# GpSimd rounds the high half of the second layer's weights from its fifth unit on; loads, splits and values of the attention stand elsewhere

## The chip, the cores and the metric

The kernel runs on one core of a Trainium2 chip. The metric is the device time of one execution in microseconds (us): the median of several executions. Five engines work at once, each through its own instructions in order: TensorE (PE, with PEld for its weight loads), VectorE (DVE), ScalarE (ACT), GpSimd (POOL) and SyncE (SP, which here only issues DMAs). They meet at semaphores.

## The reference

Three parts follow each other, on 2 sequences of 576 tokens (1152 tokens of 512 numbers):

```python
# 1: attention, 8 heads of 64, causal, with a bias from running sums
cum = np.cumsum(np.maximum(s, 0.0), axis=-1)
scores = scale * np.matmul(q, k.transpose(0, 1, 3, 2))
scores = np.where(causal, -1e9, scores + np.minimum(-(cum[..., :, None] - cum[..., None, :]), 0.0))
attn = softmax(scores);  x = np.matmul(attn, v)          # then to (1152, 512)
# 2: a layer of 2048 hidden units with ELU
h = x @ w_in;  x = np.where(h > 0, h, np.exp(np.minimum(h, 0)) - 1) @ w_out
# 3: four experts of 1024 hidden units, weighed by p
for e in range(4):
    out += p[:, e:e + 1] * (np.maximum(x @ w1[e], 0.0) @ w2[e])
```

## The kernel before

The tokens are worked in three groups: 256, 448 and 448. The first group goes alone. Its attention (`attention_first`) is done at once; then it goes through part 2 (`layer1`, 16 units of 128 hidden columns, numbers 0 to 15) and part 3 (32 units, numbers 16 to 47: `NAB` is 16, `NU` is 48). Behind the matmuls of this group the attention of the other 896 tokens is computed, piece by piece (`attention_parts`, run by `Background`). Behind the last units, the first operands of the next stage are made (`early_parts`). From about 240 us on, the two big groups go together through parts 2 and 3 (`both`); the change does not touch that.

**A slot** is one step of the loop for the first group. It runs the up product of one unit (`up1`, `up2`), then `advance(n)`, then the down product of the unit two before. Between them it calls `background(at)`, which runs as many pieces of the attention as the table of points says for that place, from slot 14 on (`BG_FROM`).

**The weights of part 3.** `fetch(n)` (L100) loads a unit's 512 KB into one of 3 buffers `raw`. `prepare(n)` (L107) writes two halves for it into one of 5 buffers `wu`: the high half is the value rounded to the matmul's type (a copy on ACT, L115), and the low half is what the rounding left off, `split_lo` (L92), a subtraction on DVE of two tiles in SBUF. PE multiplies high by high, high by low and low by high (`three`, L718). `advance(n)` (L725) fetches up to unit n+4 and prepares up to unit n+2, so a unit is prepared two slots ahead of its use.

**The attention.** `JOBS` gives eight large jobs (`jobs`, one for each pair of heads and sequence) and four small ones of 128 rows (`small`). A job has items: 128 rows of one head, or a last item of 64 rows of both heads. For an item PE computes the scores (`scores`, `qk`, L563 and L565), DVE adds the mask and takes the maximum (L605), ACT takes the exponential (L612), DVE divides (L585, in `normalise`), PE transposes (L622) three items later (`LATE`), and ACT copies the transposed block into `pt` (L640). After a job's last item, `values` (L663) multiplies with v. `split` (L548 to L551 on ACT, L92 on DVE, and two small loads of the running sums, L545) makes rounded and remaining parts of q and k for one head of a job; it is called in front of the scores of the item before the first that needs it. `load` issues a job's q, k and v in `values` of the job two before; two fills on POOL (L512 and L627) zero the rest of a last chunk.

A scheduler orders each engine's instructions from the program's order and its own estimates; the order is fixed when the program is built.

## Time and profile before

| | |
|---|---|
| median of 3 runs | 684.36 us (681.95 to 688.29) |
| the profiled execution | 683.55 us, of which the profile's span is 681.8 us |
| PE busy | 674.5 us, 99% |
| DVE busy | 583.9 us, 86% |
| ACT busy | 374.5 us, 55% |
| POOL busy | 16.1 us, 2% |
| granted TensorE clock over the span | 1.00 |

The stages in this profile: the first attention until 19 us, part 2 of the first group until 78 us, its part 3 until 240 us, the big groups until 681.8 us. The background attention runs from about 68 to 222 us. A matmul's record lasts until its result is out, while the next one has long begun, so the records overlap, and a short stall of PE is hidden under the tail of the record in front of it.

### The profile page before, as it was taken

How to read it: one execution, taken by the hardware profiler on the slowest of the kernel's cores; microseconds unless marked ns; L12 is line 12 of the kernel's file. 1: busy time of each engine (PE TensorE's matmuls, PEld its weight loads, DVE VectorE, ACT ScalarE, POOL GpSimd, SP SyncE). 2: the span in 40 equal slices, each digit the busy share in tenths (PEclk: the TensorE clock that was granted, in tenths of full speed). 3: DMA queues.
4: the chain of work that ended last, by engine and by line, in shares of the span. 5: the costliest groups of instructions: out<-in, count | busy, mean ns of one | idle time of the engine just before them, and what ended most of it. 6: DMA issues, size and time to landing. Idle time of an engine off the chain costs nothing.

```text
span 681.8 us, 9896 instructions
## 1 busy us (share of the span) xinstructions
PE 674.5 (99%) x3548; PEld 585.3 (86%) x3548; DVE 583.9 (86%) x1139; ACT 374.5 (55%) x763; POOL 16.1 (2%) x47
## 2 busy tenths in 40 slices
PE   9999899999999999999999999999999999999998
PEld 7888788888887888999999888888888888888886
DVE  7999789988977889998999999988888888888765
ACT  6998879888986759554445553333233322223220
POOL 5011000000000000000000000000000000000000
PEclk9999999999999999999999999999999999999999
DMA  8999937755333001111111112111111111110002
GB/s 300 409 365 390 253 121 214 194 169 162 117 108 107 19 31 63 62 62 62 63 62 62 62 36 89 62 62 45 35 47 61 62 62 62 62 62 0 1 0 109
DMA packets 30513, 73.55 MB, mean 108 GB/s; under 512 B 3968, under 2 KB 12544, under 8 KB 30464
## 3 DMA queue, kind: packets, MB, share of 16 engines
q1 hardware_dynamic: 29072, 68.37, 30.4%
q0 software_dynamic: 1248, 4.42, 1.6%
q8 instruction: 28, 0.46, 0.3%
q14 instruction: 21, 0.17, 0.1%
q10 hardware_dynamic: 144, 0.13, 0.1%
HBM read 66.13 MB, written 6.77 MB: 107 GB/s over the span
## 4 chain that ended last, share of the span: by engine, by line
PE 82%; DMA 8%; ACT 4%; DVE 3%; SPq 1%; issue 1%; DVEq 0%; ACTq 0%
PE acc L718 40%; PE att L1053 16%; PE up L1053 12%; PE up L718 6%; DMA pt<-in_qT 2%; PE att L663 2%; DMA wu<-in_w 2%; DMA yl<-in_w 2%; PE acc L622 1%; PE att L622 1%; PE acc L663 1%; DMA cd<-in_w 1%; DMA ox<-in_w 1%; ACT p L612 1%; SPq L145 1%
## 5 line engine op out<-in xcount | busy, mean ns | idle before, releaser
L718 PE MATMUL acc<-w,h 128*128 128x512 f32 (+1 forms) x672 | 170.1, 390 | 0.0
L718 PEld LDWEIGHTS acc<-w,h 128*128 128x128 f32 x672 | 125.9, 188 | 21.4
L1053 PE MATMUL att<-S,top 128*128 128x448 f32 x432 | 99.2, 365 | 0.1
L785 DVE SCALAR_TENSOR_TENSOR xa<-acc,pr,xa 128x512 f32<-128x512 f32 (+1 forms) x105 | 78.1, 745 | 15.2 <-PE acc L718 14.0
L1053 PEld LDWEIGHTS att<-S,top 128*128 128x128 f32 x432 | 80.7, 188 | 9.8 <-DVE u L1079 0.5
L1072 ACT ACTIVATE h<-c 128x448 fp32r<-128x448 f32 x48 | 27.5, 575 | 110.3 <-DVE c L1079 110.1
L718 PE MATMUL acc<-h,w 128*128 128x448 f32 x384 | 86.2, 364 | 0.0
L718 PEld LDWEIGHTS acc<-h,w 128*128 128x128 f32 x384 | 71.5, 188 | 7.1 <-ACT h L1069 0.3
L1053 PE MATMUL up<-x2a,top 128*128 128x448 f32 x288 | 66.3, 367 | 0.2 <-DVE top L92 0.2
L1053 PEld LDWEIGHTS up<-x2a,top 128*128 128x128 f32 x288 | 53.9, 188 | 7.0 <-DVE top L92 0.6
L718 PE MATMUL acc<-wu,gt 128*128 128x512 f32 x192 | 55.4, 403 | 0.0
L718 PE MATMUL up<-yh,wu 128*128 128x256 f32 x256 | 52.7, 287 | 0.0
L1079 DVE TENSOR_TENSOR c<-att,u 128x448 f32<-128x448 f32 x70 | 43.6, 623 | 9.5 <-PE att L1053 8.7
L1073 DVE SCALAR_TENSOR_TENSOR h<-c,h 128x448 fp32r<-128x448 f32 x48 | 29.8, 623 | 18.1 <-ACT h L1072 18.1
L92 DVE TENSOR_TENSOR wu<-raw,wu 128x1024 fp32r<-128x1024 f32 (+1 forms) x33 | 39.0, 1187 | 6.2 <-ACT wu L115 6.2
L718 PEld LDWEIGHTS up<-yh,wu 128*128 128x128 f32 x256 | 42.0, 190 | 1.9 <-issue 0.7
L1072 ACT ACTIVATE h<-up 128x448 fp32r<-128x448 f32 x16 | 8.7, 544 | 55.7 <-PE up L1053 55.7
L718 PEld LDWEIGHTS acc<-wu,gt 128*128 128x128 f32 x192 | 34.0, 189 | 4.9
L612 ACT ACTIVATE p<-p,nm 128x384 f32<-128x384 f32 (+4 forms) x56 | 34.5, 616 | 5.9 <-DVE nm L605 5.3
L718 PE MATMUL up<-yl,wu 128*128 128x256 f32 x128 | 36.5, 285 | 0.1
L1169 DVE TENSOR_TENSOR ox<-acc,ox 128x448 f32<-128x448 f32 x56 | 34.3, 618 | 2.7 <-PE acc L718 2.4
L115 ACT ACTIVATE wu<-raw 128x1024 fp32r<-128x1024 f32 (+1 forms) x33 | 33.6, 1027 | 3.2 <-PE acc L718 3.1
(234 smaller groups left out, 1217.0 us busy)
## 6 DMA issues: line engine op xcount, KB each, us to landing
raw<-in_w SPq DMA_DIRECT2D x35, 512.0 KB
wr<-in_w SPq DMA_DIRECT2D x10, 1024.0 KB
wr<-in_w SPq DMA_DIRECT2D x12, 512.0 KB
wu<-in_w SPq DMA_DIRECT2D x10, 512.0 KB
k<-in_kT SPq DMA_DIRECT2D x16, 288.0 KB
w_dec<-wu POOLq DMA_DIRECT2D x8, 512.0 KB, 7.3
wr<-w_dec SPq DMA_DIRECT2D x4, 1024.0 KB
cd<-in_w SPq DMA_DIRECT2D x6, 512.0 KB
```

The source lines that it names most:

```text
L92: return DVE.tensor_tensor(out=lo, in0=x, in1=hi.bitcast(F32), op=ALU.subtract)
L115: ACT.activation(t[:, 0, r], x[:, r], AF.Copy)
L612: ACT.activation(p, p, AF.Exp, bias=nm, scale=-1.0, accum_out=sm)
L622: PE.transpose(pt[:cb[c + 1] - cb[c], m, :], p[:, cb[c]:cb[c + 1]], ident)
L663: PE.matmul(o[64 * j:64 * j + 64, qs:nq], job["v"][:, c, 64 * j:64 * j + 64], job["pt"][:, j, c, qs:nq], start=c == 0, stop=c == n_c - 1)
L718: PE.matmul(o, a[m], b[n], start=first and i == 0, stop=last and i == 2)
L785: DVE.scalar_tensor_tensor(out=o_sb, in0=o, scalar=pr[:, i, e:e + 1], in1=o_sb, op0=ALU.mult, op1=ALU.add)
L1053: PE.matmul(bank, tops[q][:, m, op, cs], x[:, n, c], start=first and c + i == 0, stop=c == 1 and i == 2, skip_group_check=True)
L1072: ACT.activation(h[:, 0, u, cs], c, AF.Relu)
L1073: DVE.scalar_tensor_tensor(out=h[:, 1, u, cs], in0=c, scalar=0.0, in1=h[:, 0, u, cs].bitcast(F32), op0=ALU.max, op1=ALU.subtract)
L1079: DVE.tensor_tensor(out=t, in0=a, in1=b, op=ALU.add)
L1169: DVE.tensor_tensor(out=y[:, c, cs], in0=o, in1=y[:, c, cs], op=ALU.add)
```

## The change

1. `prepare`: from unit 20 on (the fifth of part 3), the high half is made by a copy on POOL in place of the copy on ACT. That is 28 of 32 units. The low half stays on DVE.
2. Loads at the start of the background attention: the running sums of the first two splits are asked for first (`load_sums`), then the small jobs' q, k and v, and then the raw weights of units 16, 17 and 18. Before, units 16 and 17 were asked for ahead of the small jobs' tensors. `advance` fetches and prepares nothing before slot 14.
3. `split` is called behind the scores of an item and for the item after the next, one item earlier than before. A job's q and k (`load_both`) are asked for right after the second split of the job two before; v (`load_values`) in `values`, as before.
4. `values` of a job stands behind the transposes of the next item; before, it stood in front of them.
5. `up2` of unit 16: the four matmuls with the low half of the activations (`yl`) come last.
6. `keep_warm(9)` in place of `keep_warm(7)`: two more matmuls without use at the start.

```diff
-                ACT.activation(t[:, 0, r], x[:, r], AF.Copy)
+                if n < NAB + 4:
+                    ACT.activation(t[:, 0, r], x[:, r], AF.Copy)
+                else:
+                    POOL.tensor_copy(t[:, 0, r], x[:, r])
...
-        keep_warm(7)
+        keep_warm(9)
...
             with tc.issue_after(last.ins):
-                fetch(fetch_at[0])
-            fetch_at[0] += 1
+                while fetch_at[0] < NAB + 3:
+                    fetch(fetch_at[0])
+                    fetch_at[0] += 1
...
+            if j == 1 and job.get("next"):
+                load_both(job["next"])
...
-            if job in jobs and jobs.index(job) + 2 < len(jobs):
-                load(jobs[jobs.index(job) + 2])
+            if job["next"]:
+                load_values(job["next"])
...
             if small:
+                load_sums(items[0])
+                load_sums(items[1])
...
-                        if c[2] and n + 1 < len(items):
-                            split(items[n + 1])
                         scores(it, c)
+                        if c[2] and n + 2 < len(items):
+                            split(items[n + 2])
...
-            if ready:
-                parts.append(ready.pop())
+            due = ready[:]
+            ready.clear()
...
+            parts += due
...
-        while fetch_at[0] <= min(n + 4, NU - 1):
+        while n > BG_FROM - 1 and fetch_at[0] <= min(n + 4, NU - 1):
...
-        while prepare_at[0] <= (NAB if n == NAB - 3 else min(n + 2, NU - 1)):
+        while n > BG_FROM - 1 and prepare_at[0] <= min(n + 2, NU - 1):
...
-            for c in range(NCC):
-                three(o, halves(t, 0, dm(c)), (yh[:, c], yl[:, c]), c == 0, c == NCC - 1)
+            terms = [(c, i) for c in range(NCC) for i in range(3)]
+            if n == NAB:
+                terms.sort(key=lambda a: a[1] == 1)
```

POOL, from the last write of decoded weights on, before (`v` and `pt` are fills of the attention's tiles, `w_dec` is a store):

```order
L188 DMA w_dec<-wu 128x1024 x8
L512 MEMSET v 64x128 x2
L627 MEMSET pt 64x2x64 x2
L512 MEMSET v 64x128
L627 MEMSET pt 64x2x64
```

and the same place in the changed kernel:

```order
L191 DMA w_dec<-wu 128x1024 x8
L515 MEMSET v 64x128 x2
L118 CAST wu<-raw 128x1024 x2
L647 MEMSET pt 64x2x64 x2
L118 CAST wu<-raw 128x1024 x3
L515 MEMSET v 64x128
L647 MEMSET pt 64x2x64
L118 CAST wu<-raw 128x1024 x3
```

The copies of units 20 and 21 come ahead of the first two fills of `pt`, those of units 22 to 24 behind them, and so on to unit 47; each waits for the fills in front of it.

PE at the first scores of the background attention (`kh,qs` and `kl,qb`), in slots 14 to 16, before (L813 is the down product of part 2, L823 its up product):

```order
L823 MATMUL up<-xf,ox 128x256 x4
L563 MATMUL att<-kh,qs 128x128
L813 MATMUL acc_467<-gt,wu 128x256
L813 MATMUL acc_468<-gt,wu 128x256
L813 MATMUL acc_469<-gt,wu 128x256
L813 MATMUL acc_470<-gt,wu 128x256
L563 MATMUL att<-kh,qs 128x128
L813 MATMUL acc_467<-gt,ox 128x256
L565 MATMUL att<-kl,qb 128x128
```

and in the changed kernel (L838, L848, L583 and L585 are the same lines of code):

```order
L848 MATMUL up<-xf,ox 128x256 x4
L838 MATMUL acc_469<-gt,wu 128x256
L838 MATMUL acc_470<-gt,wu 128x256
L838 MATMUL acc_471<-gt,wu 128x256
L838 MATMUL acc_472<-gt,wu 128x256
L583 MATMUL att<-kh,qs 128x128
L838 MATMUL acc_469<-gt,ox 128x256
L585 MATMUL att<-kl,qb 128x128
```

The first scores stand four matmuls later on PE.

SP behind the last coded weights (`xa`), before (`raw` is a unit's weights of part 3; `pt` here the small jobs' q, k and v):

```order
L145 DMA xa<-in_w 128x1024 x3
L104 DMA raw<-in_w 128x1024 x2
L478 DMA pt<-in_qT 128x4x128
L481 DMA pt<-in_kT 64x4x128 x4
L483 DMA pt<-in_v 128x512
L104 DMA raw<-in_w 128x1024
```

and in the changed kernel:

```order
L148 DMA xa<-in_w 128x1024 x3
L544 DMA qb<-rows_d 4x4x128
L544 DMA kl<-rows_d 4x4x128
L544 DMA qb<-rows_d 4x4x128
L544 DMA kl<-rows_d 4x4x128
L481 DMA pt<-in_qT 128x4x128
L484 DMA pt<-in_kT 64x4x128 x4
L486 DMA pt<-in_v 128x512
L104 DMA raw<-in_w 128x1024 x3
```

Two loads of weights moved from in front of the small jobs' tensors to behind them, and four loads of a few KB in front.

## Rows read from the trace of the kernel before

**Rows 1.** The page: busy time by engine; GB/s moved in 40 slices of 17 us.
```profile
PE 674.5 (99%) x3548; PEld 585.3 (86%) x3548; DVE 583.9 (86%) x1139; ACT 374.5 (55%) x763; POOL 16.1 (2%) x47
...
GB/s 300 409 365 390 253 121 214 194 169 162 117 108 107 19 31 63 62 62 62 63 62 62 62 36 89 62 62 45 35 47 61 62 62 62 62 62 0 1 0 109
```

**Rows 2.** Busy time by stretch: from:to, length, engines (instructions), clock, DMA share, GB/s.
```profile
95.00:140.00 45.00, 44.21 (x302) 36.92 (x304) 41.43 (x110) 41.60 (x101) 1.04 (x6) 1.00 0.69 191
140.00:222.00 82.00, 81.94 (x563) 68.25 (x559) 67.25 (x177) 67.89 (x162) 1.69 (x8) 1.00 0.43 132
222.00:240.00 18.00, 18.00 (x110) 16.00 (x109) 16.47 (x25) 12.13 (x19) 0.00 (x0) 1.00 0.02 9
```

**Rows 3.** Timeline of PE around its four longest stalls: start, us, line, idle before.
```profile
70.84 0.33 PE L563 MATMUL att<-kh,qs 128*128 128x128 f32 x1 [0.64 <-ACT kh L549]
...
75.14 0.33 PE L563 MATMUL att<-kh,qs 128*128 128x128 f32 x1 [0.68 <-DVE nm L605]
...
84.08 0.30 PE L622 MATMUL att<-ident,p 128*128 128x128 f32 x1 [0.56 <-DVE p L585]
...
105.52 0.41 PE L572 MATMUL att<-kl,qb 68*128 68x384 f32 x1 [0.53 <-ACT gt L907]
```

**Rows 4.** Timelines of SP, ACT and DVE ahead of the first two stalls.
```profile
49.97 0.99 SPq L104 DMA_DIRECT2D raw<-in_w  x2
51.07 0.42 SPq L478 DMA_DIRECT2D pt<-in_qT  x1
...
67.62 0.63 ACT L548 ACTIVATE qs<-pt 64x512 fp32r<-64x512 f32 x1 [2.51 <-DMA pt<-in_qT]
...
73.65 1.23 DVE L92 TENSOR_TENSOR wu<-raw,wu 128x1024 fp32r<-128x1024 f32 x1 [0.52 <-ACT wu L115]
74.79 0.28 DVE L605 CUSTOM_DVE_ANT_0 p<-att,mask 128x128 f32<-128x128 f32 x1
```

**Rows 5.** Waits of weight loads, 62 to 240 us: us, times, longest; those with releaser.
```profile
PEld att L563 <- DVE nm L605: 1.3, 2, 1.1
...
PEld att L663 <- ACT pt L640: 1.0, 3, 0.6
...
PEld acc L653 <- ACT pt L640: 0.2, 1, 0.2
```

**Rows 6.** POOL by line and form: count, busy us, mean ns, idle before.
```profile
L244 POOL CAST rows<-cum 16x576 fp32r<-16x576 f32 x1 | 0.7, 654 | 0.9 <-DVE cum L234 0.9
```

**Rows 7.** DVE and ACT by line and form, 95 to 222 us.
```profile
L92 DVE TENSOR_TENSOR wu<-raw,wu 128x1024 fp32r<-128x1024 f32 x23 | 28.1, 1222 | 3.7 <-ACT wu L115 3.7
L115 ACT ACTIVATE wu<-raw 128x1024 fp32r<-128x1024 f32 x23 | 24.2, 1051 | 3.2 <-PE acc L718 3.1
```

**Rows 8.** Timeline near 5 us: two equal POOL instructions, and DVE beside them.
```profile
4.89 0.42 DVE L305 TENSOR_TENSOR cump<-cum,cump 16x256 fp32r<-16x256 f32 x1
5.11 0.30 POOL L221 TENSOR_SCALAR_AFFINE_SELECT maskp<-maskp 64x64 f32<-64x64 f32 x1
5.34 0.48 DVE L231 SCALAR_TENSOR_TENSOR bias<-bias,eight 16x320 f32<-16x320 f32 x1
5.46 0.47 POOL L221 TENSOR_SCALAR_AFFINE_SELECT maskp<-maskp 64x64 f32<-64x64 f32 x1
```

**Rows 9.** DVE's time in 95:140 by line: first L92, then L585.
```profile
95.00:140.00 45.00, 18.52 (x22) 1.00 0.69 191
...
95.00:140.00 45.00, 7.59 (x18) 1.00 0.69 191
```

**Rows 10.** Timelines of POOL and PE near 100 us: fills, and unit 22's first two matmuls.
```profile
97.67 0.35 POOL L627 MEMSET pt<- 64x128 f32 x2 [33.66 <-DVE qs L92]
...
102.89 0.28 PE L718 MATMUL up<-yh,wu 128*128 128x256 f32 x1
103.01 0.28 PE L718 MATMUL up<-yl,wu 128*128 128x256 f32 x1
```

**Rows 11.** Timeline of PE at the start of the program.
```profile
0.78 3.33 PE L389 MATMUL att<-const-float32-0.0 128*128 128x128 f32 x14 [0.78 <-PEq L1266]
```

More of the change, by code (lines that the diff above doesn't have):

```diff
@@ L521, in load, with of, load_sums @@
                                                 in_=v[b, cb[i]:cb[i + 1], r])
+        for i, job in enumerate(jobs):
+            job["next"] = jobs[i + 2] if i + 2 < len(jobs) else None
+        def of(it):
+            job, j = it["job"], 1 if it["j"] is None else it["j"]
+            return job, j, small if job["q1"] == 128 else [job]
+        def load_sums(it):
+            job, j, together = of(it)
+            heads = slice(job["b"] * H + 2 * together[0]["hp"] + j,
+                          job["b"] * H + 2 * together[-1]["hp"] + j + 1, 2)
+            job[j, "sums"] = []
+            for tag, r, a in (("qb", slice(0, 4), job["q0"]), ("kl", slice(2, 6), 0)):
+                t = sb([68, len(together) * (job["q1"] - a)], tag, 2, F32R)
+                job[j, "sums"].append(t)
+                with late():
+                    SP.dma_start(
+                        out=t[64:].bitcast(F32).rearrange("r (h n) -> r h n", h=len(together)),
+                        in_=rows_d[heads, r, a:job["q1"]].rearrange("h r n -> r h n"))
         def split(it):
-            job, j = it["job"], 1 if it["j"] is None else it["j"]
+            job, j, together = of(it)
             if (j, "q") in job:
                 return
+            if (j, "sums") not in job:
+                load_sums(it)
             mine, other = (slice(64 * i, 64 * i + 64) for i in (j, 1 - j))
-            together = small if "all" in job else [job]
-            heads = slice(job["b"] * H + 2 * together[0]["hp"] + j,
-                          job["b"] * H + 2 * together[-1]["hp"] + j + 1, 2)
             if "all" in job:
@@ L540, in split @@
             kh = sb([128, k.shape[-1]], "kh", 2, F32R)
-            qb = sb([68, q.shape[-1]], "qb", 2, F32R)
-            kl = sb([68, k.shape[-1]], "kl", 2, F32R)
-            for t, r, a in ((qb, slice(0, 4), job["q0"]), (kl, slice(2, 6), 0)):
-                with late():
-                    SP.dma_start(
-                        out=t[64:].bitcast(F32).rearrange("r (h n) -> r h n", h=len(together)),
-                        in_=rows_d[heads, r, a:job["q1"]].rearrange("h r n -> r h n"))
+            qb, kl = job[j, "sums"]
             ACT.activation(qs[mine], q, AF.Copy)
@@ L683, in start @@
                 for job in jobs[:2]:
-                    load(job)
+                    load_both(job)
+                    load_values(job)
             split(items[0])
```

24 lines of the change are left out of this document (14 added, 10 removed).

## The prediction

> **What bounds the kernel now.** I read the page first. PE is busy for 674.5 of 681.8 us [rows 1], and its clock is granted in full in every stretch below. The number and size of useful matmuls stay the same, so this change can only take away time in which PE stands, or add some. Next I looked at the stretches: from 140 to 222 us PE is busy for 81.94 of 82 us, from 222 to 240 for all 18, and from 95 to 140 for 44.21 of 45 [rows 2]. So the attention behind part 3 is hidden, and what can be won lies early, between 70 and 110 us. The reader is to see in the timeline of PE its four longest stalls: 0.64 us at 70.84, 0.68 at 75.14, 0.56 at 84.08 and 0.53 at 105.52 [rows 3]. They make 2.41 us. A matmul's record lasts beyond the start of the next (one of 0.28 us is followed after 0.12 us [rows 10]), so each stall is about 0.16 us longer than its bracket; I take 3.05 us for the four. The waits of the weight loads, which also show what hides under a tail, name a releaser for 7.7 us in 14 lines between 62 and 240 us, the four stalls among them [rows 5]. That is about the most that the change can win.
>
> The second thing to see is how full the helpers are. From 95 to 140 us DVE works 41.43 and ACT 41.60 of 45 us; from 140 to 222 us they work 67.25 and 67.89 of 82; from 222 to 240 us 16.47 and 12.13 of 18 [rows 2]. DVE has 3.57, 14.75 and 1.53 us left.
>
> **The copy on POOL.** One copy takes 1.05 us on ACT [rows 7]. The trace has no copy of 128x1024 on POOL. Its nearest row is a conversion of the same kind over 576 columns, 0.654 us [rows 6], which scaled by columns is 1.16 us; that is the upper end, since a fixed part would not scale. ACT's own 1.05 us is the lower. I take 1.1 us. 28 copies leave ACT, 29 us in all, and POOL takes 31 us of a queue that had 16 us in all [rows 1]. The 32 units take 162 us (78 to 240), 5 us each, so POOL keeps up. The last eight copies, with no fill between them, can even run ahead of ACT's old times.
>
> ACT is not what PE waits for from 110 us on, so most of the 29 us buys nothing. It buys something where ACT's queue makes PE or DVE late: DVE waits 3.7 us in all for these copies [rows 7], and the stall at 105.52 us ends behind ACT.
>
> **What the copy costs DVE.** Here the trace speaks against the change. Near 5 us POOL runs two equal instructions on 64x64 elements [rows 8]. The first takes 0.30 us, the second 0.47 us. Beside the second, DVE runs an instruction with two inputs in SBUF from 5.34 to 5.82 us, and POOL ends at 5.93, just behind it. The first likewise ends at 5.41, just behind a DVE subtraction that ends at 5.31. So the two engines seem to exclude each other there. The Trainium skill (SBUF — State Buffer, Who interferes with whom) says that a DVE instruction with two SBUF inputs and a GpSimd instruction that reads SBUF block each other fully, whoever starts first; by that rule each copy may hold DVE for its whole length, and the trace agrees as far as these two rows go.
>
> The price here: while a copy holds, DVE can go on until its next subtraction of SBUF tiles. In 95:140 these subtractions (L92) fill 18.52 of 45 us, and the divisions of the probabilities (L585) another 7.59 [rows 9]. Whether the latter collide no row shows. If only L92 does, a copy costs DVE 0.41 x 1.1 = 0.45 us; with both 0.58 x 1.1 = 0.64 us. The bounds are 0 (POOL waits each time, which harms nobody, as units are ready some us early) and 1.1 us. I take 0.6. Nine copies fall in 95:140, fourteen in 140:222, three in 222:240, two before. At 0.6 DVE needs 5.4 us more where it had 3.57, 8.4 where it had 14.75, 1.8 where it had 1.53: 2.1 us too much. Scores are three items ahead of their transposes, and DVE has room again behind 140 us, so not all of a late DVE reaches PE. I take **+1.4 us**.
>
> **Loads in another order.** The small jobs' tensors stand behind 1 MB of weights that is not needed until 78 us [rows 4]. ACT waits 2.51 us for them and starts the first split at 67.62 us; at the 390 GB/s of the fourth slice (51 to 68 us) [rows 1] 1 MB is 2.7 us. So the first split can start some 2.5 us earlier. Behind the loads stand the weights of units 16 to 18; the total ahead of the large jobs' loads is the same. On PE the first scores now also stand behind four down products, so the 0.64 us stall has cover from both sides. The second stall has another cause: DVE makes the low half of unit 17 at 73.65 us, itself waiting 0.52 us for ACT, and the maximum for which PE waits comes only at 74.79 [rows 4]. In the changed order the first maxima stand in front of that subtraction. I count both stalls gone: 0.64 + 0.68 + 2 x 0.16, **-1.6 us**.
>
> **Splits earlier, values later.** The stall at 105.52 us is at a score whose operands come from ACT late in a full queue [rows 3]. The split is called one item earlier and ACT is freer: **-0.7 us**. The stall at 84.08 us waits for the division of a first item; that chain starts earlier but has the same length: half of it, **-0.35 us**. `values` in front of the next transposes waits 1.0 us in three times for ACT's copy of the last block [rows 5]; behind them, ACT has that time. With the other small waits (14 lines, 7.7 us, less some 4.6 in the four stalls and the loads around them) some 3 us are left; I count a third, **-1.1 us**. Unit 16's `yl` matmuls last: a wait of 0.3 us among these. The q and k loads that move cost nothing: they are covered by the two items of lead.
>
> **Two more warm matmuls.** Seven are 14 records in 3.33 us [rows 11], so two more are four records, 0.95 us. Below, 0: the first sums come from DVE and may be the later ones. I take **+0.3 us**.
>
> **The sum.** -1.6 - 0.7 - 0.35 - 1.1 + 0.3 + 1.4 = -2.05 us. The profiled execution took 683.55 us, so 681.5; its time lies 0.8 us under the median of the runs, so I state the forecast against the median: 684.36 - 2.05 = **682.3 us**.
>
> **The rivals.** *DVE becomes the bound.* If a copy holds DVE for its whole 1.1 us, DVE needs 9.9, 15.4 and 3.3 us more in the three stretches, 6.3 + 0.65 + 1.8 = 8.8 us above what it had left. If PE then waits for all of it, and only the two early stalls go: 684.36 + 8.8 + 0.3 - 1.6 = **691.9 us**. For it speaks the second select [rows 8]; against it that POOL must find DVE between two subtractions, and that DVE's own idle time has waits for ACT in it that go away. It decides from about 0.7 us a copy on, where the loss equals the gain. Chance 0.12.
>
> *All waits go.* If all 7.7 us of waits with a releaser vanish [rows 5] and DVE is not held, 684.36 - 7.7 + 0.3 = **677.0 us**. Against it: waits of a full pipeline move more often than they vanish. Chance 0.12.
>
> *Nothing happens.* The stalls go and come back in other places, since PE's order is new throughout and DVE is as late as ACT was before: 684.4 us, give or take 1.5. Chance 0.2.
>
> *POOL's queue is late.* The copies of units 22 to 24 stand behind two fills that ended at about 98.0 us before [rows 10]. A copy (1.1) and a subtraction (1.22) later it is 100.4 us, and unit 22's first matmul came at 102.89. Even a fill 2.5 us later only meets PE; beyond that PE loses us for us: at 6 us late, some 3.5 us, 685.8. Chance 0.06; it ends within 1%.
>
> **How the numbers follow.** The forecast (0.5) and the rivals make one: 0.5 + 0.12 + 0.12 + 0.2 + 0.06. About 1% (6.8 us) is what a measurement of this kernel can tell from no change. Under 677.5 lies the second rival, over 691.2 the first; the rest is within 1%: 0.12, 0.76, 0.12. The range reaches to the all-waits case and to a lock that costs 0.9 us a copy: 676.5 to 690.0 us. The forecast's own range is 679.5 to 685.
>
> **What would show it.** POOL: 28 copies of 1.05 to 1.2 us, some longer because they wait behind DVE. DVE: subtractions of 128x1024 with means well over 1.22 us, and busy over 43 of 45 us early on. PE: no stall over 0.5 us from 68 to 77 us, stalls between 77 and 110 us of half their sum, and no more than 1.5 us between 110 and 240 us. ACT: some 4 us less for every 20 us until 240 us. The forecast is wrong if PE shows new waits for DVE of more than 3 us behind 95 us, if the copies take 2 us, or if anything behind 245 us moves.

## The result and the profile after

The changed kernel takes 688.93 us (median of 10 runs, 687.41 to 689.76); the kernel before took 683.52 us beside it. The ratio is 1.0071, with a 95% interval from 1.0056 to 1.0087: **0.7% slower**, where 682.3 us was forecast. That is within the 1% that was called no change, and inside the range, but on the other side of the old time and 6.6 us from the forecast.

The page after (span 686.3 us), busy times beside [rows 1], and the chain of work that ended last, by engine:

```profile
PE 677.0 (99%) x3552; PEld 585.4 (85%) x3552; DVE 592.9 (86%) x1139; ACT 350.2 (51%) x735; POOL 50.9 (7%) x75
...
PE 72%; DVE 15%; ACT 5%; DMA 4%; issue 3%; DVEq 0%; SPq 0%; ACTq 0%
```

The same chain in the kernel before:

```profile
PE 82%; DMA 8%; ACT 4%; DVE 3%; SPq 1%; issue 1%; DVEq 0%; ACTq 0%
```

DVE's share of it has risen from 3 to 15%. Busy time by stretch in the changed kernel (the columns of [rows 2]: PE, PEld, DVE, ACT, POOL), with the stretch of the first two stalls ahead:

```profile
62.00:78.00 16.00, 15.89 (x78) 13.59 (x76) 11.56 (x34) 11.32 (x28) 0.52 (x3) 1.00 1.07 307
95.00:140.00 45.00, 42.89 (x304) 36.08 (x302) 43.25 (x103) 33.34 (x86) 11.73 (x15) 1.00 0.62 184
140.00:222.00 82.00, 80.22 (x543) 66.04 (x543) 70.59 (x181) 55.53 (x149) 17.31 (x22) 1.00 0.44 128
222.00:240.00 18.00, 17.34 (x105) 13.67 (x103) 14.61 (x19) 8.64 (x15) 5.82 (x3) 1.00 0.09 29
```

From 62 to 78 us PE now stands for 0.11 us: the early stalls [rows 3] are gone. From 95 to 140 us PE has lost 1.3 us of work against [rows 2], and from 140 to 222 us, where it had stood for 0.06 us, it now stands for 1.8. ACT is 8 and 12 us emptier in these two stretches, and it did not help. DVE is fuller, 43.25 of 45 us and 70.59 of 82, with no instruction more (its page count is 1139, as before).

The same as a running account: how much later than in the kernel before the same matmul starts, in us (from the two traces; "unit n" is the first up product of unit n of part 3):

| place (us before) | changed kernel |
|---|---|
| first up product of part 2 (19.3) | +1.00 |
| last down product of part 2 (78) | -0.70 |
| unit 24 (117) | +0.55 |
| unit 32 (162) | -0.02 |
| unit 43 (224) | +2.67 |
| end of part 3 (240) | +4.20 |
| end | +4.58 |

So the start loses 1.0, the stretch from 20 to 78 us wins 1.7, and then three stretches lose: 1.25 up to unit 24, 2.7 between units 32 and 43, and 1.5 in the last units. Between units 24 and 32 the changed kernel loses nothing; behind part 3 it loses 0.4.

Two of these pieces are those of one execution only. The start of part 2 differs from profile to profile: over all kernels of this document its first up product comes between 0.23 us earlier and 1.00 later than in the kernel before with nine warm matmuls, and between 0.31 earlier and 0.60 later with seven. And up to unit 24 two kernels with the same order of instructions there (the change with seven warm matmuls, and with its last four copies on ACT, both below) lose 2.4 and 2.7 us where the changed kernel loses 1.25. The 2.7 between units 32 and 43 are the same in all three.

Which instructions got longer is seen in DVE's groups by line and form from 78 to 246 us; the first two rows are of the order edits with the copies left on ACT (the first experiment), the next two of the changed kernel (x count | busy us, mean ns | idle before):

```profile
L92 DVE TENSOR_TENSOR kl<-k,kh 64x576 fp32r<-64x576 f32 x16 | 12.0, 748 | 0.3
L599 DVE TENSOR_SCALAR sm<-sm 128x2 f32<-128x2 f32 x27 | 4.4, 162 | 5.2 <-ACT p L629 5.1
```

```profile
L92 DVE TENSOR_TENSOR kl<-k,kh 64x576 fp32r<-64x576 f32 x16 | 14.3, 894 | 0.3
L602 DVE TENSOR_SCALAR sm<-sm 128x2 f32<-128x2 f32 x27 | 7.5, 279 | 4.4 <-ACT p L632 4.4
L603 DVE RECIPROCAL sm<-sm 128x2 f32<-128x2 f32 x27 | 4.3, 161 | 0.4
L92 DVE TENSOR_TENSOR wu<-raw,wu 128x1024 fp32r<-128x1024 f32 x30 | 36.4, 1216 | 1.4 <-POOL wu L118 1.0 <-ACT wu L116 0.4
```

The subtractions of k and the additions to the softmax sums have means up by 146 and 117 ns; the reciprocals and the large weight subtractions have not. Wherever I speak of *lengthening* below, it is the sum, over DVE's instructions from 78 to 246 us, of what each takes over the median of the same operation and form without POOL copies, where that is more than 0.05 us. For the changed kernel it is 11.3 us in 21 instructions, the longest single one 0.84 us: **0.40 us a copy**.

### The profile page after: what moved, and what is told of

Read it like the earlier page. It is cut to its first block, busy times and chain, and to the rows that moved or that the text cites. A ratio compares the mean times of both kernels' runs of the same rounds, so it can differ in the third digit from the quotient of the medians.

```text
span 686.3 us, 9910 instructions
## 1 busy us (share of the span) xinstructions
PE 677.0 (99%) x3552; PEld 585.4 (85%) x3552; DVE 592.9 (86%) x1139; ACT 350.2 (51%) x735; POOL 50.9 (7%) x75
## 4 chain that ended last, share of the span: by engine, by line
PE 72%; DVE 15%; ACT 5%; DMA 4%; issue 3%; DVEq 0%; SPq 0%; ACTq 0%
PE acc L743 35%; PE att L1082 16%; PE up L1082 12%; DVE wu L92 3%; DVE p L625 2%; PE up L933 2%; DVE p L605 2%; DMA k<-in_kT 2%; DVE kl L92 1%; DMA pt<-in_kT 1%; ACT z L177 1%; DVE qs L92 1%; DMA xa<-in_w 1%; PE att L683 1%; DVE gt L937 1%
## 5 line engine op out<-in xcount | busy, mean ns | idle before, releaser
L118 POOL CAST wu<-raw 128x1024 fp32r<-128x1024 f32 x28 | 33.9, 1213 | 97.6 <-PE acc L743 57.9
L92 DVE TENSOR_TENSOR wu<-raw,wu 128x1024 fp32r<-128x1024 f32 (+1 forms) x33 | 38.9, 1184 | 2.1 <-ACT wu L116 1.1
```

The costliest lines, as they stand in the source:

```text
L92: return DVE.tensor_tensor(out=lo, in0=x, in1=hi.bitcast(F32), op=ALU.subtract)
L118: POOL.tensor_copy(t[:, 0, r], x[:, r])
```

## The experiments

Each expectation was written before its run. The names in them: READ LOCK or LOCK, DVE's instructions on SBUF are held while POOL reads SBUF; START, the two warm matmuls shift everything; LATE HALF, the rounded half is ready too late; DVE BOUND, each us more on DVE costs PE a us; SLACK, DVE's idle time takes it; CHAIN, only time in the softmax chain counts; BURSTS, only long single waits count; ORDER, in the first four expectations that the moved splits, loads and values themselves cost, and in those of the last runs that the planner (the scheduler) put instructions in another succession, because copies on POOL leave ACT free in its plan. The ratios are against the kernel before, run beside each set; its medians are 683.52 us in the first section and for the change, and 683.82 to 683.91 in the others. So a difference of two runs from different sets is uncertain by some 0.4 us.

### Which part of the change costs

**Copies back on ACT, all else changed.**

```diff
-                if n < NAB + 4:
-                    ACT.activation(t[:, 0, r], x[:, r], AF.Copy)
-                else:
-                    POOL.tensor_copy(t[:, 0, r], x[:, r])
+                ACT.activation(t[:, 0, r], x[:, r], AF.Copy)
```

> The changed kernel with the 28 rounded halves made by ACT again; everything else of the change stays. Theory LOCK (POOL's copies hold DVE's subtractions and divisions, and PE then waits for DVE): 688.9 less the 5.9 us that the trace of the change lost behind 78 us, so 683.0 to 684.5; DVE beside no POOL work goes back to 1.22 us for 128x1024 and 0.75 us for 64x576 in every instance. Theory ORDER (the moved splits, loads and values put PE's pieces where they wait): 688 to 689, POOL's copies cost nothing. Theory START (two more warm matmuls shift everything by 1.0 us): the start stays 1.0 us late in this run under both.

Measured: 681.69 us, ratio 0.9969 [0.9957, 0.9981]. The copies on POOL cost 688.93 - 681.69 = **7.2 us**; everything else together wins 1.8. More comes back than LOCK expected (683.0 at the least), and the start of part 2 is 0.36 us late in this profile, not 1.0.

**The kernel before with POOL's copies alone** (the opposite edit, in the old order of loads and splits).

> The kernel before with one edit: POOL makes the rounded halves from the fifth unit of part 3 on. Theory LOCK: 683.5 plus 4 to 6 us, 687.5 to 689.5, with DVE instructions of two SBUF inputs lengthened beside the copies and those that read PSUM not. Theory ORDER: 683 to 684.5, since nothing but the engine of the copies moves.

Measured: 689.94 us, ratio 1.0100 [1.0082, 1.0117]; lengthening 12.2 us. The copies cost 6.4 us there too, 0.4 us more than LOCK's range, so it is not their meeting with the new order of loads and splits.

**The change with seven warm matmuls.**

```diff
-        keep_warm(9)
+        keep_warm(7)
```

> The changed kernel with seven warm matmuls at the start as before. Theory START: 1.0 us less than the changed kernel, 687.9, and part 2's first up product at 19.3 us in place of 20.3. If the warm matmuls only shift a wait that is there anyway, 688.9.

Measured: 688.08 us, ratio 1.0063 [1.0051, 1.0075]. By the medians the two warm matmuls cost 0.85 us. The two profiled executions, 688.36 us with seven and 688.10 with nine, do not show it.

**The order edits alone**: copies on ACT and seven warm matmuls.

> The loads, splits and values of the change with neither POOL's copies nor the two warm matmuls. LOCK and START together: 683.5 less the 1.7 us won between 62 and 78 us, 681 to 683. ORDER: 687.5 to 688.

Measured: **680.85 us**, ratio 0.9959 [0.9948, 0.9971]. This is faster than both kernels, and 0.15 us under the range that was expected. Between it and the first run the two warm matmuls cost 0.84 us by the medians of five runs each. In the mean of all profiles part 2 starts 0.44 us later with nine warm matmuls than with seven, so their cost lies between about 0.4 and 0.85 us. From 140 to 222 us PE is busy throughout, and the early stalls are gone:

```profile
62.00:78.00 16.00, 15.90 (x79) 13.60 (x78) 11.53 (x33) 11.30 (x29) 0.41 (x2) 1.00 1.08 295
140.00:222.00 82.00, 82.00 (x563) 68.28 (x560) 67.91 (x178) 68.16 (x163) 1.39 (x8) 1.00 0.45 133
```

### What about the copies costs: late, or in DVE's way?

**A spare copy in the kernel before**: ACT makes the rounded half as ever; POOL copies the same tile once more into the place of the low half, which DVE then overwrites.

```diff
                 ACT.activation(t[:, 0, r], x[:, r], AF.Copy)
+            if n >= NAB + 4:
+                POOL.tensor_copy(t[:, 1, r], x[:, r])
```

> The kernel before, ACT still making the rounded halves; beside that POOL copies each unit's raw weights (from unit 20 on) into the place of the low half, which DVE's subtraction then overwrites. Nothing useful is moved. Theory READ LOCK (a POOL instruction that reads SBUF and a DVE instruction that reads two SBUF tensors exclude each other, and PE waits for the late DVE): 683.5 plus 5 to 8 us, 688.5 to 691.5, DVE instructions lengthened by 10 to 13 us in sum. Theory LATE HALF (the loss comes from weights that are ready late because POOL's queue stands in front of the subtraction): the same loss here and in the run with fills.

Measured: 690.62 us, ratio 1.0091 [1.0061, 1.0121]; lengthening 15.5 us, where 10 to 13 was expected. The order on ACT, DVE and PE is line for line that of the kernel before, and nothing that a matmul reads comes from POOL. But DVE's subtraction has to wait for the spare copy, since it overwrites it, so this run alone does not tell the lock from that wait. The next one does.

**A spare fill**: the same with `POOL.memset(t[:, 1, r].bitcast(F32), 0.0)` in the copy's place. The subtraction waits for it in the same way.

> As the run before, but POOL fills that place with zeros (it only writes, 128x1024) in place of copying. READ LOCK: subtractions are not lengthened; at most the divisions of SBUF by a scalar are, so 683.5 to 685.5. LATE HALF: as with the copies, 688 to 691, since the subtraction waits for POOL in the same way.

Measured: 684.42 us, ratio 0.9995 [0.9976, 1.0014]. The order is again that of the kernel before. DVE's groups from 78 to 246 us, as above:

```profile
L92 DVE TENSOR_TENSOR kl<-k,kh 64x576 fp32r<-64x576 f32 x16 | 11.9, 746 | 0.7 <-ACT kh L551 0.4
L584 DVE TENSOR_SCALAR sm<-sm 128x2 f32<-128x2 f32 x26 | 8.0, 307 | 3.3 <-ACT p L614 3.2
```

Not one subtraction of two SBUF tiles is longer (64x576: 748 ns in the mean without POOL's work, 746 here, where nine of the 16 meet a fill). Some of the additions to the sums (159 ns alone, seven of the 26 here between 418 and 865) and some divisions still are, 6.2 us in all. So POOL has to read SBUF to hold a subtraction. DVE idles for the fills as long as for the copies (1.5 us in two times, 1.3 in one), and yet the time is only 0.55 us over that of the kernel before, which the interval does not tell from nothing: LATE HALF falls as the main cause of the 6.7 us, and READ LOCK stands.

**More DVE work that the planner knows of.** First 28 subtractions of 128x256 (0.42 us each, 11.7 us) ahead of the units' low halves; then 28 multiplications by 1.0 of up to 128x384 (9.0 us in its trace) between reciprocal and division in the softmax. Both in the kernel before, without work for POOL.

```diff
+            if n >= NAB + 4:
+                split_lo(t[:, 1, 0:256], x[:, 0:256], x[:, 0:256])
```

> The kernel before with a subtraction of 128x256 more on DVE for each unit from 20 on, in front of the unit's own subtraction, which overwrites it: 28 x 0.42 = 11.7 us of DVE, about what the copies cost it, and no POOL. Theory DVE BOUND (between 78 and 245 us what DVE does more reaches PE for the most part, though DVE stands 15 to 20 percent of that time): 683.5 plus 5 to 8 us. Theory SLACK (my reckoning before the run: DVE's idle time takes it): 683.5 to 685.5.

Measured: 685.23 us, ratio 1.0015 [0.9998, 1.0032].

```diff
             DVE.reciprocal(sm, sm)
+            m = norm[-1][:, :min(384, norm[-1].shape[-1])]
+            DVE.tensor_scalar(m, m, 1.0, None, op0=ALU.mult)
```

> The kernel before, with one more DVE multiplication by 1.0 of up to 128x384 (about 0.42 us, 28 of them, 11 us or a little less in all) in the chain of each pair of softmax rows, between the reciprocal and the divisions; GpSimd has no new work. The DVE time is that of the earlier kernel with 28 more subtractions ahead of the weight splits, which lost 1.3 us; only the place differs. CHAIN (time on DVE counts when it stands in the chain from maximum to division to transposes, on which PE waits; that is where the lock falls): a loss of 4 to 6 us, 688 to 690. BURSTS (only the size of single waits counts, 0.42 us is absorbed wherever it stands): 685 to 686.

Measured: 683.71 us beside 683.91, ratio 0.9990 [0.9978, 1.0003]. DVE BOUND and CHAIN fall: 11.7 us more on DVE cost 1.4, which the interval does not quite tell from nothing, and 9.0 us cost nothing, which is less than BURSTS expected too. But in both kernels the planner also changed the order of DVE and PE around the new instructions. Whether time that the planner knows of is absorbed because it is planned for, or because no piece is over 0.42 us, these two runs do not show. In the profile of the first, 0.8 of the 2.5 us are lost ahead of 78 us, where DVE has no new work yet.

**Copies in quarters**, in the changed kernel.

```diff
-                    POOL.tensor_copy(t[:, 0, r], x[:, r])
+                    for c in range(0, 1024, 256):
+                        POOL.tensor_copy(t[:, 0, c:c + 256], x[:, c:c + 256])
```

> The changed kernel with each copy on POOL cut into four of 256 columns. If the two engines exclude each other for one whole instruction, DVE waits at most 0.3 us for each in place of 1.05; DVE's lengthening should fall from 11.3 us to 5 to 8 us and the time from 688.9 to 685.5 to 687.5. If POOL takes the turn again for each quarter ahead of DVE, or more turns cost what shorter ones win, 688 to 690.

Measured: 687.86 us, ratio 1.0048 [1.0033, 1.0064], between the two ranges that were expected. The lengthening falls to 6.2 us and no single one is over 0.25 us, so DVE is held for the length of POOL's instruction, not for the tile. Only 1.1 us comes back, though: four quarters take longer than one copy (1.44 us in this row), and DVE, whose next instruction in line is that unit's subtraction, now idles for them, 4.9 us in eight times against 1.0 in two. Timeline of POOL, then of DVE, in this kernel:

```profile
194.86 1.44 POOL L119 CAST wu<-raw 128x256 fp32r<-128x256 f32 x4 [1.79 <-issue]
...
196.33 1.22 DVE L92 TENSOR_TENSOR wu<-raw,wu 128x1024 fp32r<-128x1024 f32 x1 [0.50 <-POOL wu L119]
197.47 0.68 DVE L606 TENSOR_SCALAR p<-p,sm 128x256 f32<-128x256 f32 x2
```

The division behind it is what PE's transposes wait for, 0.5 us at 199.14. The run shows the lock's form; it doesn't measure its price.

### Where it is lost, and by which way

**Copies of the last four units back on ACT**, the rest changed.

```diff
-                if n < NAB + 4:
+                if n < NAB + 4 or n >= NU - 4:
                     ACT.activation(t[:, 0, r], x[:, r], AF.Copy)
```

> The changed kernel with the copies of the last four units (44 to 47) back on ACT. In the changed kernel those of 45 to 47 ran 1.9 to 2.0 us on GpSimd and their splits ended 1.3, 0.4 and 1.0 us behind the start of the unit's first up product, where before they ended 0.3 to 1.6 us ahead of it; the stretch from 222 us to the end of the third part lost some 1.5 us. If these late copies are what the end of the stage loses, the median falls by 1.2 to 1.8 us, to about 687.3, and no up product behind 222 us waits for DVE's L92 more than 0.2 us. If the end loses by something else, 688.7 to 689.2.

Measured: 686.99 us, ratio 1.0041 [1.0024, 1.0058], 1.9 us below the change. From unit 43 to the end of part 3 it loses 0.0 us (the changed kernel 1.5). This loss is late copies after all: timeline of POOL, DVE and PE at the end of part 3 in the changed kernel:

```profile
226.72 1.88 POOL L118 CAST wu<-raw 128x1024 fp32r<-128x1024 f32 x1 [6.58 <-PE acc L743]
229.53 1.92 POOL L118 CAST wu<-raw 128x1024 fp32r<-128x1024 f32 x1 [0.93 <-PE acc L743]
232.35 2.02 POOL L118 CAST wu<-raw 128x1024 fp32r<-128x1024 f32 x1 [0.90 <-PE acc L743]
...
230.81 1.53 DVE L92 TENSOR_TENSOR top<-ox,top 128x512 fp32r<-128x512 f32 x2
232.25 1.21 DVE L92 TENSOR_TENSOR wu<-raw,wu 128x1024 fp32r<-128x1024 f32 x1
...
233.52 0.51 PE L933 MATMUL up<-yh,wu 128*128 128x256 f32 x2 [0.54 <-DVE wu L92]
```

The copies take 1.9 to 2.0 us here instead of 1.04, beside DVE's long instructions with two SBUF inputs: it is POOL's turn to be held. The weight slots come free only as PE ends a unit, so there is no time ahead, and the split of unit 45 at 232.25 is late by what PE then stands.

**Without the addition of 1e-9** to the softmax sums (28 instructions of 128x2, which leave a sum of at least 1 as it is), with seven warm matmuls: once with the copies on POOL, once on ACT.

```diff
-            DVE.tensor_scalar(sm, sm, 1e-9, None, op0=ALU.add)
             DVE.reciprocal(sm, sm)
```

> The changed kernel with seven warm matmuls and without the addition of 1e-9 to the sums of the softmax (28 instructions of 128x2, which leave a sum of at least 1 as it is). These additions were the instructions that met a copy most often: 12 of 28, 159 ns alone, 429 ns in the mean beside one. Without them the lock has 3.3 of its 11.3 us less to fall on, and the chain is 28 x 0.16 us shorter. ADDITIONS CARRY IT: the distance to the same kernel with the copies on ACT falls from 7.2 us to 4 or less, so about 684. ANY INSTRUCTION WILL DO (the lock then holds the next two-input or SBUF instruction): the distance stays at 6.5 to 7.2, so 687 to 688.

> The order edits alone (copies on ACT, seven warm matmuls), without the same 28 additions of 1e-9: the other half of the pair. 4.5 us of DVE time go from the chain of the softmax. CHAIN: where 0.42 us more per pair costs much, 0.16 us less should give something back, 0.5 to 1.5 us below 680.85, so 679.4 to 680.4. BURSTS and SLACK: PE waits there for nothing that 0.16 us shortens, 680.6 to 680.9.

Measured: 684.72 us, ratio 1.0012 [1.0003, 1.0021], and 681.76, ratio 0.9968 [0.9955, 0.9980]. With the additions gone the copies cost 3.0 us instead of 7.2, as ADDITIONS CARRY IT says; but the lengthening fell only from 11.5 to 9.6 us, since divisions took the hold that the additions no longer took, and without the additions the order on DVE and PE changed as well (the stall of 1.2 us at 183 us, below, is 0.6). So the pair does not show that the additions carry it. The second kernel is 0.9 us slower than with the additions (680.85), outside both ranges that were expected for it; since its order changed too, it says nothing on CHAIN or SLACK.

**Only ten copies on POOL**, those of units 25 to 34, in the stretch where the changed kernel lost nothing.

```diff
-                if n < NAB + 4:
+                if not NAB + 9 <= n < NAB + 19:
                     ACT.activation(t[:, 0, r], x[:, r], AF.Copy)
```

> The changed kernel with only the copies of units 25 to 34 on GpSimd (10 of 28; they ran from 113 to 162 us), the others on ACT. In that stretch the changed kernel had the most lengthening of DVE (4.3 us between 117 and 160 us) and lost nothing there against the copies on ACT (0.05 us from unit 24 to unit 32). If the place decides (DVE has room in this stretch), 681.5 to 682.5. If each copy costs its share of 7.2 us, 684.3.

Measured: 682.20 us, ratio 0.9970 [0.9950, 0.9989], 0.5 us over the copies on ACT where the share of ten copies would be 2.6. The lengthening is 4.7 us, and it costs PE 0.7 us by the running account. So the place counts for more than the us of lengthening.

**LOCK without the new succession**: the order edits with nine warm matmuls and the copies on ACT (681.69), plus a spare copy on POOL as above. The order on ACT, DVE and PE is line for line that of the first run.

> The order edits with nine warm matmuls and the copies on ACT (681.69 measured), and GpSimd copies each of the 28 tiles once more into the place of the low half, ahead of DVE's subtraction. The order on ACT, DVE and PE is line for line that of the kernel without the spare copies; only GpSimd works more. LOCK: the loss of the change and more, as with the spare copies in the kernel before (6.7 us there), 687 to 689. ORDER: the lock alone costs less than half of 7.2, so 683.5 to 685. If the two causes add up, this loss and that of the kernel with fills make about 7.

Measured: 689.59 us, ratio 1.0072 [1.0047, 1.0096]: **7.9 us** for the lock, 0.6 us more than its range. Since the two kernels have the same succession, an instruction can be set beside itself. DVE, and then PE, first with the copies on ACT alone:

```profile
99.17 0.15 DVE L599 TENSOR_SCALAR sm<-sm 128x2 f32<-128x2 f32 x1
99.36 0.49 DVE L92 TENSOR_TENSOR qs<-q,qs 64x320 fp32r<-64x320 f32 x1
...
99.96 0.73 DVE L92 TENSOR_TENSOR kl<-k,kh 64x576 fp32r<-64x576 f32 x1
100.62 0.84 DVE L602 TENSOR_SCALAR p<-p,sm 128x576 f32<-128x576 f32 x2
...
101.27 0.63 PE L639 MATMUL att<-ident,p 128*128 128x128 f32 x4
```

and with the spare copies (POOL first):

```profile
99.51 2.03 POOL L117 CAST wu<-raw 128x1024 fp32r<-128x1024 f32 x2
102.72 1.33 POOL L117 CAST wu<-raw 128x1024 fp32r<-128x1024 f32 x1 [1.19 <-DVE kl L92]
...
100.26 0.31 DVE L601 TENSOR_SCALAR sm<-sm 128x2 f32<-128x2 f32 x1
100.60 1.27 DVE L92 TENSOR_TENSOR qs<-q,qs 64x320 fp32r<-64x320 f32 x1
...
101.99 0.73 DVE L92 TENSOR_TENSOR kl<-k,kh 64x576 fp32r<-64x576 f32 x1
102.64 1.61 DVE L604 TENSOR_SCALAR p<-p,sm 128x576 f32<-128x576 f32 x2
...
103.29 0.63 PE L641 MATMUL att<-ident,p 128*128 128x128 f32 x4 [0.94 <-DVE p L604]
```

Two copies run from 99.51 to 101.54. The addition and the subtraction of q that fall beside them take 0.31 and 1.27 us where they took 0.15 and 0.49. What DVE does between 101.9 and 102.7 us, with no copy beside it, takes what it took (the subtraction of k 0.73 us). Two divisions meet the next copy and take 0.77 us more. Together 1.7 us of lengthening in one chain; 0.94 us of it reaches PE, where no wait was shown before.

**The new succession without the lock on subtractions**: the changed kernel with fills in the place of the 28 copies (the rounded halves of these units are left out of the computation).

```diff
-                    POOL.tensor_copy(t[:, 0, r], x[:, r])
+                    POOL.memset(t[:, 0, r].bitcast(F32), 0.0)
```

> The changed kernel with a fill by GpSimd in the place of each of its 28 copies (the rounded halves of those units are left out of the computation). The order on ACT, DVE and PE is nearly that of the changed kernel (12 to 41 lines differ; with the copies on ACT it is 75 to 94), so ACT has the same instructions in the same succession, but a fill does not lengthen DVE's subtractions, and the earlier run with fills lost only 0.5 us. ORDER (what costs is the succession that was planned with ACT free of the copies: q and k copies ahead of the exponent and of the eviction on which PE waits): the stall of 1.2 us at 183 us stays, the stretch from unit 32 to unit 43 loses about 3 us as in the changed kernel, and the time is 684.5 to 686. LOCK (what costs is DVE lengthened by the copies): nearly all comes back, 681.7 to 682.5.

Measured: 683.10 us, ratio 0.9985 [0.9971, 0.9999]; lengthening 3.1 us. That lies between the two ranges: neither cause alone is it. The kernel is 1.4 us over the copies on ACT and **5.8 us** under the change. Up to unit 32 it loses nothing (it is 0.55 us ahead); all its loss lies between units 32 and 43, the largest piece 1.07 us at 180.46. What stands there on ACT, with the copies on ACT (first run):

```profile
176.56 0.62 ACT L629 ACTIVATE p<-p,nm 128x384 f32<-128x384 f32 x1
...
177.17 0.58 ACT L657 ACTIVATE pt<-acc 128x512 f32<-128x512 f32 x1
177.65 0.71 ACT L629 ACTIVATE p<-p,nm 128x512 f32<-128x512 f32 x1
...
178.62 0.65 ACT L654 ACTIVATE pt<-acc 128x256 f32<-128x256 f32 x2
...
179.49 0.58 ACT L563 ACTIVATE qs<-q 64x448 fp32r<-64x448 f32 x1
```

and in the changed kernel, with PE's stall:

```profile
179.61 0.58 ACT L660 ACTIVATE pt<-acc 128x512 f32<-128x512 f32 x1
180.22 0.57 ACT L566 ACTIVATE qs<-q 64x448 fp32r<-64x448 f32 x1
180.81 0.69 ACT L567 ACTIVATE kh<-k 128x576 fp32r<-128x576 f32 x1
181.41 0.71 ACT L632 ACTIVATE p<-p,nm 128x512 f32<-128x512 f32 x1
...
182.38 0.65 ACT L657 ACTIVATE pt<-acc 128x256 f32<-128x256 f32 x2
...
183.07 0.44 PE L583 MATMUL acc<-kh,qs 128*128 128x384 f32 x1 [1.04 <-ACT pt L657]
```

With ACT free of the weight copy, the planner has put the next job's q and k copies, 1.2 us, ahead of the exponent and of the eviction that frees the accumulator for which PE waits. With fills the succession at this place is the same and so is the stall, and DVE has no lengthened instruction between 160 and 194 us there. ORDER is real, and in the changed kernel it is the smaller part. The lock can make such a stall by itself, though: with the spare copies, in the succession of the copies on ACT, PE stands 0.9 us one score earlier, at 183.42, behind a division that was held at 180.18.

**Undoing that one place**: in the changed kernel the q and k copies have to stand behind the last exponent written ahead of them.

```diff
-            ACT.activation(qs[mine], q, AF.Copy)
-            ACT.activation(kh, k, AF.Copy)
+            with tc.issue_after(last_exp[0].ins) if last_exp else nullcontext():
+                ACT.activation(qs[mine], q, AF.Copy)
+                ACT.activation(kh, k, AF.Copy)
...
-                ACT.activation(p, p, AF.Exp, bias=nm, scale=-1.0, accum_out=sm)
+                last_exp[:] = [ACT.activation(p, p, AF.Exp, bias=nm, scale=-1.0, accum_out=sm)]
```

> The changed kernel, where ACT's copies of the next job's q and k have to stand behind the last exponent that was written ahead of them. In the changed kernel they ran at 180.2 to 181.4 us ahead of the exponent at 181.4, and PE stood 1.2 us at 183.07 for an eviction behind it. ORDER: that stall goes and others like it shrink, 1 to 2.5 us faster than the changed kernel (688.93), 686.4 to 688. LOCK: no change, 688.5 to 689.3.

Measured: 698.83 us, ratio 1.0204 [1.0174, 1.0235], 9.9 us slower than the change; both expectations missed. The rule holds at every split, not at the one, and now scores wait for their operands (14 stalls of up to 1.2 us ahead of `kh,qs` and `kl,qb` matmuls between 100 and 220 us). It says how much depends on the succession, and nothing on the price of that one place.

### What the runs add up to

How much later than the kernel before the same matmul starts, us, cumulated:

| place | change | copies on ACT | change with fills (ORDER) | copies on ACT and spare copies (LOCK) |
|---|---|---|---|---|
| last down product, part 2 | -0.70 | -1.34 | -1.60 | -0.95 |
| unit 24 | +0.55 | -1.24 | -1.78 | +1.47 |
| unit 32 | -0.02 | -1.86 | -2.41 | +1.64 |
| unit 43 | +2.67 | -2.39 | -0.57 | +4.57 |
| end of part 3 | +4.20 | -2.38 | -0.60 | +5.87 |

The change's 7.2 us are, in nearly its own succession (with the fills 12 to 41 lines of an engine's order differ, as the expectation says), 1.4 us of ORDER (683.10 - 681.69) and 5.8 us that go when POOL stops reading (688.93 - 683.10), of which 1.5 lie in the last three units, where copies and DVE hold each other up. If each kernel is taken against its own runs of the kernel before, the two parts are 1.1 and 6.1 us; by the running accounts of the profiles they are 1.8 and 5.2. The 1.4 us also include whatever the fills' 3.1 us of lengthening cost. The loss up to unit 24 is the lock's alone: with fills there is none.

The two causes do not add up: in the succession of the copies on ACT the lock alone costs 7.9 us, and with the 1.4 of ORDER that would be 9.3, where about 7 was expected. So 5.8 us is the lock's price in the changed kernel, and not its price in any order.

Open: the price of a us of lengthening. By the account at the end it was 0.58 us of PE with the spare copies in the new order (8.3 us by 14.2), 0.40 in the old (6.1 by 15.5), 0.15 with the ten copies (0.7 by 4.7) and 0.09 with the spare fills (0.6 by 6.2). The size of a single hold is not it: the spare fills held single instructions by up to 0.70 us. It seems to hang on which instruction meets which copy, and I have no rule that gives it beforehand.

## Why the prediction was wrong, point by point

**The copy on POOL.** The trace has the copies' own times:

```profile
L118 POOL CAST wu<-raw x28: 1037/1049/2016, 84.2 to 232.4; 128x1024 fp32r<-128x1024 f32 x28
```

(minimum, median and longest ns). 1.1 us was near enough, and POOL does keep up, except at the end: that the last eight copies "can even run ahead of ACT's old times" was false, since they wait for PE's slots, as ACT's copies had, and then take 2 us. I had read POOL's idle queue as a lead, and taken ACT's relief for a small gain that costs nothing. It cost some 1.4 us (ORDER, above), because it moved ACT's instructions. ACT's order is fixed when the program is built, so the place behind 140 us could have been read before the forecast. The rival *POOL's queue is late* came true in another place than it named: not at units 22 to 24, but in the last three. Between them DVE waits for a copy only twice, 0.5 us each, at 185.7 and 206.6 us.

**What the copy costs DVE: the step that failed.** +1.4 us was forecast, 7.2 was measured, of which 5.8 are the lock's. The lock itself was foreseen, and its size was not what failed: 0.6 us a copy was taken, 0.40 is there, and the small instructions that I left out (128x2, 162 ns) are in it with 3.2 of 11.3 us, while the 128x1024 subtractions, which I named as the sign, hardly meet a copy, as each runs right behind its own. Wrong was the second half of the step: to set the sum against DVE's idle time in a stretch, 3.57, 14.75 and 1.53 us, and to let only two thirds of the 2.1 us of excess reach PE. By that reckoning 0.40 us a copy would have cost 0.03 us from 95 to 140 us (nine copies) and nothing from 140 to 222 us (14 copies, 5.6 us, into 14.75 idle) or later. The stretch from 140 to 222 us cost most. DVE's idle us stand where DVE waits for ACT or PE (in the kernel before, 7.7 and 4.6 of these 14.75 us), and an instruction that is held delays everything behind it in a fixed order; the next idle moment gives it back to DVE, but PE may have needed it first. The changed kernel shows one such place, the lengthened addition and, four instructions later, PE's wait:

```profile
213.62 1.04 POOL L118 CAST wu<-raw 128x1024 fp32r<-128x1024 f32 x1 [7.05 <-PE acc L743]
...
213.91 0.77 DVE L602 TENSOR_SCALAR sm<-sm 128x2 f32<-128x2 f32 x1 [0.91 <-ACT p L632]
214.59 0.55 DVE L625 CUSTOM_DVE_ANT_0 p<-att,mask 128x384 f32<-128x384 f32 x1
...
215.15 1.20 DVE L92 TENSOR_TENSOR wu<-raw,wu 128x1024 fp32r<-128x1024 f32 x1
216.27 0.78 DVE L605 TENSOR_SCALAR p<-p,sm 128x576 f32<-128x576 f32 x2
...
216.92 0.52 PE L642 MATMUL acc<-ident,p 128*128 128x128 f32 x3 [0.44 <-DVE p L605]
```

The addition takes 0.61 us over its 0.16, DVE had been idle 0.91 us just before it, and PE stands 0.61 us from its usual pace at 216.92. The idle time was of no use, because it came before. One place shows the path; that all of the 5.8 us went this way is argued from it and from the runs without reads, and was not traced stall by stall.

The rival *DVE becomes the bound*, at 0.12, came nearer: it had PE wait for a DVE that the copies hold. But it reckons by idle time as well. "From about 0.7 us a copy" is where that reckoning turns, and the loss came at 0.40, in a kernel where DVE is not the bound: 9.0 and 11.7 us more of planned work on DVE cost nothing and 1.4 us.

The Trainium skill (SBUF — State Buffer, Who interferes with whom) says that a DVE instruction with two SBUF inputs contends with a GpSimd instruction that reads SBUF and not with one that only writes it, and it counts scalar operations among those that can, under conditions on their operands, take the shared ports by themselves. The runs agree with both halves: subtractions with two SBUF inputs are held by POOL's copies (64x576: 894 ns in the mean for 748) and not by its fills (746); scalar operations from SBUF to SBUF are held by both (128x2: up to 0.77 us by copies in the changed kernel and 0.87 by the spare fills, for 0.16). The maxima, which read PSUM, are held by neither (128x384: 545 to 552 ns in the mean in the changed kernel, with the spare fills and with the copies on ACT).

**Loads in another order.** Right: -1.6 forecast, -1.7 measured between 20 and 78 us, both stalls gone, by the copies-on-ACT kernels as well (-1.70, -1.71).

**Splits earlier, values later.** -2.15 forecast for 84.08, 105.52 and the rest. With the order edits alone the place from 78 us to the end of part 3 wins 1.1 us (-1.29 to -2.35). The direction holds, the size was twice too large: the splits' chains and the planner give some of it back early (up to unit 24 they win nothing, +0.12).

**Two more warm matmuls.** +0.3 forecast, +0.84 and +0.85 by the medians of two pairs, +0.44 by the start of part 2 in the mean of all profiles. The bounds, 0 and 0.95, held it; the +0.3 was too small, since half or more of the four records is paid for. Which wait decides it was not traced.

**The sum.** With what the runs showed: -1.7 (loads) - 1.1 (splits) + 0.85 (warm) + 7.2 (copies) = +5.25; measured +5.4. The first two are from profiles and the others from medians. The edits other than the copies were forecast at -3.45 and gave -1.8; the copies were forecast at +1.4 and gave +7.2. The sign hung on the latter. That the time lies inside the range is partly luck: its upper end was set for a lock of 0.9 us a copy, and the lock was 0.40.

**The signs.** Of those named ahead, the copies' length, DVE's 43.25 of 45 us, the quiet stretch from 68 to 77 us and ACT's relief came as told. The stalls from 77 to 110 us did not halve: PE, idle there for 1.46 us before, is idle for 2.19 (1.16 with the copies on ACT). From 110 to 240 us, where at most 1.5 us was expected, it is idle for 2.59 (0.06 before). What was to make the forecast wrong is there: three copies take 1.9 to 2.0 us, PE waits for DVE behind 95 us for 3.2 us in five lines (the three longest here, and one wait for ACT: us in all, times, longest), and what stands behind 245 us moved by 0.4.

```profile
PE att L642 <- DVE p L605: 1.3, 1, 1.3
PE acc L583 <- ACT pt L657: 1.0, 1, 1.0
PE acc L642 <- DVE p L605: 1.0, 2, 0.5
PE up L933 <- DVE wu L92: 0.5, 1, 0.5
```

The second line is ORDER's stall, the fourth that of the late copies; the first and third are waits for divisions, as the lock makes them. The four make 3.8 us; I did not place the rest of the loss stall by stall.

## What to carry to other kernels

Before work is handed to GpSimd to relieve another engine, list which of DVE's instructions on SBUF will run beside it, the small ones too, and ask of each whether PE waits behind it in DVE's fixed order; DVE's idle share of the stretch did not give the price here. Ask also what the engine that is relieved will do with the time: where a planner sets the order, a lighter ACT means another succession, which is to be read beforehand at the places where PE stands closest. When a change has several parts, run each alone: here the order edits without the copies are the best kernel, 680.85 us.

## What the runs showed of the hardware

- A DVE instruction of 128x2 elements, 0.16 us alone, took up to 0.77 us beside a copy on POOL in the changed kernel. It is held until about the end of POOL's instruction: over all runs no single hold was over 0.88 us beside copies of mostly 1.04 us, or over 0.25 beside quarters.
- It works in both directions: a POOL copy of 128x1024 that takes 1.04 us by itself took 1.9 to 2.0 us beside DVE's additions and subtractions of up to 128x896 with two SBUF inputs.
- Fills by POOL held additions and divisions from SBUF to SBUF (seven additions took 418 to 865 ns for 159) and no subtraction of two SBUF tiles.
- Reciprocals from SBUF to SBUF (128x2, 161 ns in the mean) were not held: in the changed kernel one took 0.15 us at 84.38, inside the copy from 84.24 to 85.28 us, and one 0.16 us at 219.74, inside that from 219.10 to 220.14.
